# One tile shape for the attention sum's last four matmuls, and a new search in the planner that orders an attention and two-layer MLP kernel

## The chip, the cores and the metric

One NeuronCore of a Trainium2 chip runs the whole program. The metric is the device time of one execution in microseconds (us). The profiled execution is another one, with its own time, and its trace gives start and length of every instruction.

## The reference

Thresholded attention over 4 batches x 8 heads, 576 queries and keys, head size 64, then two MLPs over 2304 tokens (512 wide, 2048 hidden). All in float32.

```python
scores = q @ k.T / 8
scores = where(scores >= max(scores) - tau, scores, -1e9)
x = softmax(scores) @ v                      # 2304 x 512
h = x @ w_in;  x = (max(h, 0) + log1p(exp(-abs(h)))) @ w_out    # first MLP
h = x @ w2_in; out = max(h, 0)**2 @ w2_out                      # second MLP
```

## The kernel before

**Tiles.** The attention is cut into 32 units. A unit is two heads of one half of a batch's queries (288 queries); four units make one token group of 288 tokens, and there are eight groups. The first MLP works on a group at a time in eight steps of 256 hidden columns (`m1_up`, `m1_split`, `m1_down`), 12 slots behind the attention (LAG). The second MLP follows in blocks of 512 tokens.

**Numbers in two parts.** A product in the MLPs is made of three matmuls of type float32r: high part by high part, low by high, high by low (L463 to L465 up, L494 to L496 down, L603 to L605 in the second MLP). The parts are split by ScalarE (a copy to float32r) and by DVE or GpSimd (the difference: L324 for weights, L344 and L345 for q and k, L482 for the hidden activations). The attention's products of weights and values stay float32; each of those matmuls shows up in the trace as two passes.

**A unit on TensorE.** `a_scores` makes the scores (L364 with 64 rows, two heads side by side; L369 with all rows). After the threshold and exp (`a_max`, `a_soft`, on DVE and ScalarE) `a_out` sums: L420 multiplies by v into `X`, 64 columns a head; L427 multiplies by ones (`one_t`, 32 columns) into `D`, which gives the denominators. Both run over 512 keys. The last 64 keys of the two heads share one 128-row slot of the tile, so the last piece of `a_out` has four matmuls of 64 rows each, in the order L432, L433, L432, L433:

```python
for o, h in enumerate(half):      # half: rows 0-63, rows 64-127
    PE.matmul(X[h], vt[h, 512:], e[h, 4], start=False, stop=True)
    PE.matmul(D[64 - 64 * o:96 - 64 * o], one_t[h], e[h, 4], start=False, stop=True)
```

L432 has 64 rows by 64 columns, L433 64 rows by 32 columns. `X` and `D` are two PSUM banks. Rows 0-63 write partitions 0-63 of `X` and 64-95 of `D`; rows 64-127 write partitions 64-127 of `X` and 0-31 of `D`. In this text these four are the slot.

**The planner.** Nothing is issued when it is written. `P.add` records an operation with its engine, an assumed duration in ns, what it reads and writes, and a key. `emit` turns the records into one order per engine: `forward` lists them by key as they come free, `backward` lists them from the end and gives new keys, and the two take turns 24 times; the shortest plan is issued. Each engine then takes its instructions strictly in that order. A flag `lock` says that GpSimd's work and some DVE work exclude each other in the plan. `emit` is called twice: once for attention with the first MLP's first 57 up steps, once for the rest. The assumed time of the slot is 590 ns, that of L420 and L427 is 490 ns a piece, with 100 more for a first piece.

Of the kernel before, what the change touches and what calls it, by code (L numbers as in the profile page):

```python
# [2 lines left out]

# [6 lines left out]
F32 = mybir.dt.float32  # L10
# [3 lines left out]
ALU = mybir.AluOpType  # L14
AX = mybir.AxisListType

B, H, S, D = 4, 8, 576, 64
# [9 lines left out]
LAG = 12  # L27
# [5 lines left out]
GPOOL = range(8, 56)  # L33
# [4 lines left out]
def f32(ap):  # L38
    return ap.bitcast(F32)


class Plan:
# [24 lines left out]
        deps.discard(i)  # L67
        self.ops.append((eng, ns, fn, deps, key, nbytes, lock or eng == "POOL"))

    def emit(self, rounds=24):  # L70

        first, n = len(self.done), len(self.ops)
        state = self.free, self.bus, self.lock
        self.done += [None] * (n - first)
        users = [[] for _ in range(n - first)]
        for i in range(first, n):  # L80
            for d in self.ops[i][3]:
                if d >= first:
                    users[d - first].append(i)
        keys = [op[4] for op in self.ops[first:]]
        best = None
        for r in range(rounds):
            self.free, self.bus, self.lock = dict(state[0]), *state[1:]
            order = self.forward(first, users, keys)
            length = max(self.free.values())
            if best is None or length < best[0]:  # L90
                best = length, order, self.done[first:], (self.free, self.bus, self.lock)
            keys = self.backward(first, users, order)
        _, order, self.done[first:], (self.free, self.bus, self.lock) = best
        for _, _, i in order:
            self.ops[i][2]()
# [122 lines left out]
def kernel(ctx: ExitStack, tc: tile.TileContext, qT, kT, vp, tau, w1i, w1o, w2i, w2o, out):  # L218
    nc = tc.nc
    w1i, w1o, w2i, w2o = (w.bitcast(U32) for w in (w1i, w1o, w2i, w2o))  # L220
    PE, ACT, DVE, POOL, SP = nc.tensor, nc.scalar, nc.vector, nc.gpsimd, nc.sync
# [35 lines left out]
    P = Plan()  # L257
    att = ExitStack()
    ap = att.enter_context(tc.tile_pool(name="att", bufs=1))
# [6 lines left out]
    k_h, k_l = (ap.tile([128, KW], F32R, name=f"k_{n}") for n in "hl")  # L266
# [7 lines left out]
    NX = 5  # L274
    xf_t = many(NX, [128, HALF], "xf")
    w_t = ap.tile([128, 18], F32, name="w_t")
    one_t = ap.tile([128, 32], F32, name="one_t")
    POOL.memset(one_t, 1.0)
    m_d = [dram.tile([18, 32], F32, name=f"m_d{i}") for i in range(4)]


# [4 lines left out]
    class Weights:  # L286
# [7 lines left out]
        def load(self, src, f, outw, key=None, pe=False):  # L294
            s = self.i % self.n
            self.i += 1
            raw, t = self.raw[s], self.t[s]
            R, T = ("wraw", id(self), s), ("wt", id(self), s)
            p, j = divmod(f, 2)
            hi, lo = (woh, wol) if outw else (wih, wil)  # L300
            W = ("wo" if outw else "wi", p, j)
            if outw:
                P.add("SP", 600, lambda: SP.dma_start(raw.rearrange("p e w -> p (e w)"), src[f * 128:(f + 1) * 128, :]), [], [R], key, 1 << 19)
                hf, lf, t2 = hi[p][:, j], lo[p][:, j], t
            else:
                P.add("SP", 600, lambda: SP.dma_start(raw.rearrange("p e w -> p (e w)"), src[f]), [], [R], key, 1 << 19)
                hf, lf = (x[p][:, :, 128 * j:128 * j + 128] for x in (hi, lo))
                t2 = t.rearrange("p (k f) -> p k f", k=4)
            low, high = raw[:, :, 0], raw[:, :, 1]
            P.add("ACT", 560, lambda: ACT.activation(f32(t), f32(high), AF.Prelu, scale=2.0 ** -112, alpha=-2.0 ** 32), [R], [T], key)  # L310
            P.add("DVE", 340, lambda: DVE.tensor_scalar(low, low, 29, None, op0=ALU.logical_shift_right), [], [R], key, lock=True)
            P.add("DVE", 610, lambda: DVE.scalar_tensor_tensor(out=t, in0=t, scalar=3, in1=low, op0=ALU.logical_shift_left, op1=ALU.bitwise_or), [R], [T], key, lock=True)
            P.add("ACT", 510, lambda: ACT.copy(hf, f32(t2)), [T], [W], key)
            if pe:
                bank, BK = h_ps[self.i // 2 % 2], ("h", self.i // 2 % 2)

                def mms():
                    PE.matmul(bank, ident, f32(t), start=True, stop=False)
                    PE.matmul(bank, negid, hf, start=False, stop=True)
                P.add("PE", 1300, mms, [T, W], [BK], key)  # L320
                b2 = bank if outw else bank.rearrange("p (k f) -> p k f", k=4)
                P.add("ACT", 530, lambda: ACT.copy(lf, b2), [BK], [W], key)
                return
            P.add("POOL", 1240, lambda: POOL.tensor_tensor(lf, f32(t2), f32(hf), op=ALU.subtract), [T], [W], key)  # L324


    def a_load(u, key):
# [10 lines left out]
    def a_prep(u, key):  # L338
        if u < RAW:
            return  # L340
        k_r, q_r, KR, QR = k_rt[u % 2], q_rt[u % 2], ("k_r", u % 2), ("q_r", u % 2)
        P.add("ACT", 330, lambda: ACT.copy(q_h, q_r), [QR], ["q_h"], key)
        P.add("ACT", 630, lambda: ACT.copy(k_h, k_r), [KR], ["k_h"], key)
        P.add("POOL", 750, lambda: POOL.tensor_tensor(q_l, q_r, f32(q_h), op=ALU.subtract), [QR, "q_h"], ["q_l"], key)  # L344
        P.add("POOL", 1520, lambda: POOL.tensor_tensor(k_l, k_r, f32(k_h), op=ALU.subtract), [KR, "k_h"], ["k_l"], key)  # L345

    def a_scores(u, key):

# [59 lines left out]
    def a_out(u, key):  # L408
        cold = COLD if u < NCOLD else 1
        e, E = st_t[u % 3], [("st", u % 3, o) for o in range(2)]  # L410
        vt, V = v_t[u % 2], ("v", u % 2)
        xf, XF = xf_t[u % NX], ("xf", u % NX)
        rb, RB = rb_t[0], "rb"
        half = [slice(0, 64), slice(64, 128)]
        X, D = a_ps[0][:, :HALF], a_ps[1][:, :HALF]
        AX0, AD = ("a", 0), ("a", 1)
        for c in range(4):
            def mms(c=c):
                for o in range(2):
                    PE.matmul(X[64 * o:64 * o + 64], vt[:, 256 * o + 64 * c:256 * o + 64 * c + 64], e[:, 5 * o + c], start=(c == 0), stop=False)  # L420
            P.add("PE", (490 + 100 * (c == 0)) * cold, mms, E + [V], [AX0], key)
        for c in range(0, 4, 2):
            def mms(c=c):
                for o in range(2):
                    for i in range(2):
                        a = 64 - 64 * o + 32 * i
                        PE.matmul(D[a:a + 32], one_t, e[:, 5 * o + c + i], start=(c == 0), stop=(c == 2 and i == 1))  # L427
            P.add("PE", (490 + 100 * (c == 0)) * cold, mms, E, [AD], key)

        def mms():  # L430
            for o, h in enumerate(half):
                PE.matmul(X[h], vt[h, 512:], e[h, 4], start=False, stop=True)  # L432
                PE.matmul(D[64 - 64 * o:96 - 64 * o], one_t[h], e[h, 4], start=False, stop=True)  # L433
        P.add("PE", 590 * cold, mms, [E[0], V], [AX0, AD], key)
        P.add("ACT", 310, lambda: ACT.copy(xf, X), [AX0], [XF], key - 0.5)
        for o in range(2):
            P.add("ACT", 310, lambda o=o: ACT.copy(rb[half[o]], D[half[1 - o]]), [AD], [RB], key - 0.5)

        d, DN = d_t[u % 2], ("d", u % 2)
        P.add("DVE", 380, lambda: DVE.tensor_reduce(d[:, 0], rb.rearrange("p (b i) -> p b i", i=32), axis=AX.X, op=ALU.max, apply_transpose=True), [RB], [DN], key + 1)  # L440
        for a in range(4):
            b = a ^ 1
            P.add("ACT", 220, lambda a=a, b=b: ACT.copy(d[32 * a:32 * a + 32, 1], d[32 * b:32 * b + 32, 0]), [DN], [("d2", u % 2)], key + 0.5)
        P.add("DVE", 140, lambda: DVE.scalar_tensor_tensor(out=d[:, 0], in0=d[:, 0], scalar=1e-9, in1=d[:, 1], op0=ALU.add, op1=ALU.add), [("d2", u % 2)], [DN], key + 1)
        P.add("DVE", 140, lambda: DVE.reciprocal(d[:, 0], d[:, 0]), [], [DN], key + 1)
        P.add("DVE", 380, lambda: DVE.transpose(rb, d[:, 0].unsqueeze(2).to_broadcast([128, 9, 32])), [DN], [RB], key + 1)
        P.add("DVE", 375, lambda: DVE.tensor_tensor(xf, xf, rb, op=ALU.mult), [RB], [XF], key + 1, lock=True)
# [28 lines left out]
            P.add("DVE", 370, lambda j=j, h=h, a=a: DVE.scalar_tensor_tensor(out=gt_t[j], in0=h, scalar=0.0, in1=a, op0=ALU.max, op1=ALU.add), [("h", j), A], [("gt", j)], key - 0.2)  # L476

    def m1_split(key):
        eng, e, ns = ("POOL", POOL, 750) if key - LAG in GPOOL else ("DVE", DVE, 375)
        for j in range(2):  # L480
            P.add("ACT", 330, lambda j=j: ACT.copy(g_hl[0][j], gt_t[j]), [("gt", j)], [("g_h", j)], key - 0.2)  # L481
            P.add(eng, ns, lambda j=j: e.tensor_tensor(g_hl[1][j], gt_t[j], f32(g_hl[0][j]), op=ALU.subtract), [("gt", j), ("g_h", j)], [("g_l", j)], key - 0.2, lock=True)  # L482
# [211 lines left out]
```

## Time and profile before

| | |
|---|---|
| median of 3 runs | 1174.6 us (1174.29 to 1176.4) |
| the profiled execution's own time | 1177.02 us |
| its span, first to last instruction | 1175.2 us |
| TensorE (PE) busy | 1145.8 us, 98% |
| DVE busy | 698.6 us, 59% |
| ScalarE (ACT) busy | 690.8 us, 59% |
| GpSimd (POOL) busy | 245.6 us, 21% |
| granted TensorE clock, mean | 0.988 |

The profiled execution lies 2.4 us over the median. A busy share is a mean over the span; the attention ends at about 706 us, and DVE, ScalarE and GpSimd do most of their work before that. A matmul is listed with its whole length, and the next begins before it ends, so what a matmul costs TensorE is read as the time from its start to the next one's start.

### The profile page before, as it was taken

Reading aid. Unit: us, or ns where it says so; the run is one execution under the profiler, and the core shown is the slowest. Engines: PE = TensorE matmul, PEld = TensorE weight load, DVE = VectorE, ACT = ScalarE, POOL = GpSimd, SP = SyncE. Lnnn points to the kernel's source line nnn. Section 1 sums busy time; section 2 is a strip of 40 time slices with the busy share of each in tenths; the row PEclk is TensorE's granted clock in tenths of the full one; section 3 lists DMA queues with packets and bytes.
Section 4 is the critical chain, followed back from the end, with each engine's and each line's share of the span. In section 5 each row is a group of like instructions: output and inputs, shape, how many; then the busy total and the mean of one; then the engine's idle time right before and its main releaser. Section 6 shows DMA issues by size and latency. Waiting matters only on the chain.

```text
span 1175.2 us, 18185 instructions
## 1 busy us (share of the span) xinstructions
PE 1145.8 (98%) x6992; PEld 887.8 (76%) x6992; DVE 698.6 (59%) x992; ACT 690.8 (59%) x1640; POOL 245.6 (21%) x209
## 2 busy tenths in 40 slices
PE   7779999999999999999999999999999999999998
PEld 3335777877877877877777879988888888888887
DVE  5999986766776666657656745889322322222232
ACT  6787887777777776777677657865322222222222
POOL 1024223332332232333223211444000000000000
PEclk9888999999999999999999999999999999999999
DMA  5365422112112112112111004765010010000010
GB/s 190 109 200 181 140 89 84 46 44 81 46 39 83 41 45 83 39 48 74 47 48 42 31 11 146 212 205 159 7 66 1 1 54 1 1 37 1 1 37 19
DMA packets 39291, 81.85 MB, mean 70 GB/s; under 512 B 6180, under 2 KB 14884, under 8 KB 39204
## 3 DMA queue, kind: packets, MB, share of 16 engines
q1 hardware_dynamic: 39204, 80.69, 21.6%
q8 instruction: 55, 0.90, 0.3%
q14 instruction: 32, 0.26, 0.1%
HBM read 71.17 MB, written 9.50 MB: 69 GB/s over the span
## 4 chain that ended last, share of the span: by engine, by line
PE 90%; DVE 4%; ACT 3%; DMA 1%; issue 0%; SPq 0%; ACTq 0%; DVEq 0%
PE h_ps L463 12%; PE h_ps L464 11%; PE h_ps L465 11%; PE y_ps L494 6%; PE y_ps L604 6%; PE y_ps L603 6%; PE y_ps L605 6%; PE y_ps L496 5%; PE y_ps L495 5%; PE a_ps L364 5%; PE a_ps L420 5%; PE a_ps L432 3%; PE a_ps L433 3%; PE a_ps L427 3%; DVE st L402 1%; PE a_ps L369 1%
## 5 line engine op out<-in xcount | busy, mean ns | idle before, releaser
L482 POOL TENSOR_TENSOR g_l<-gt,g_h 128x288 fp32r<-128x288 f32 x96 | 102.8, 1074 | 316.4 <-ACT g_h L481 278.8
L463 PE MATMUL h_ps<-x_h,wih 128*128 128x288 f32 x512 | 160.1, 313 | 0.7 <-DVE gt L476 0.7
L494 PE MATMUL y_ps<-g_h,woh 128*128 128x288 f32 x512 | 158.2, 309 | 0.0
L464 PE MATMUL h_ps<-x_l,wih 128*128 128x288 f32 x512 | 150.5, 294 | 1.2 <-DVE x_l L454 1.2
L465 PE MATMUL h_ps<-x_h,wil 128*128 128x288 f32 x512 | 151.6, 296 | 0.0
L496 PE MATMUL y_ps<-g_l,woh 128*128 128x288 f32 x512 | 151.1, 295 | 0.0
L495 PE MATMUL y_ps<-g_h,wol 128*128 128x288 f32 x512 | 150.9, 295 | 0.0
L402 DVE TENSOR_TENSOR st<-st,mb 64x288 f32<-64x288 f32 (+1 forms) x128 | 129.0, 1022 | 3.3 <-DMA mb<-m_d 2.2
L583 ACT ACTIVATE r<-h_ps 128x512 f32<-128x512 f32 (+1 forms) x80 | 44.5, 556 | 146.2 <-PE h_ps L465 145.8
L584 DVE SCALAR_TENSOR_TENSOR r<-h_ps,r 128x512 f32<-128x512 f32 (+1 forms) x80 | 51.0, 638 | 131.8 <-ACT r L583 131.6
L464 PE MATMUL h_ps<-y_l,wih 128*128 128x512 f32 (+1 forms) x320 | 120.1, 375 | 0.1
L590 ACT CAST g_h<-r 128x512 fp32r<-128x512 f32 (+1 forms) x80 | 46.2, 578 | 125.4 <-PE y_ps L604 125.4
L463 PE MATMUL h_ps<-y_h,wih 128*128 128x512 f32 (+1 forms) x320 | 119.2, 372 | 0.0
L465 PE MATMUL h_ps<-y_h,wil 128*128 128x512 f32 (+1 forms) x320 | 118.7, 371 | 0.0
L591 DVE TENSOR_TENSOR g_l<-r,g_h 128x512 fp32r<-128x512 f32 (+1 forms) x80 | 51.7, 646 | 110.9 <-ACT g_h L590 110.8
L604 PE MATMUL y_ps<-wol,g_h 128*128 128x512 f32 x288 | 114.1, 396 | 0.0
L603 PE MATMUL y_ps<-woh,g_h 128*128 128x512 f32 x288 | 114.1, 396 | 0.0
L605 PE MATMUL y_ps<-woh,g_l 128*128 128x512 f32 x288 | 114.0, 396 | 0.0
L463 PEld LDWEIGHTS h_ps<-x_h,wih 128*128 128x128 f32 x512 | 96.4, 188 | 21.9 <-issue 18.7
L494 PEld LDWEIGHTS y_ps<-g_h,woh 128*128 128x128 f32 x512 | 96.4, 188 | 16.4 <-issue 15.3
L405 DVE SCALAR_TENSOR_TENSOR st<-st,thr 128x1152 f32<-128x1152 f32 (+1 forms) x64 | 104.1, 1628 | 0.1
L476 DVE SCALAR_TENSOR_TENSOR gt<-h_ps,a_t 128x288 f32<-128x288 f32 x128 | 57.4, 450 | 77.3 <-ACT a_t L475 73.9
(102 smaller groups left out, 2410.5 us busy)
## 6 DMA issues: line engine op xcount, KB each, us to landing
k_r<-in_kT SPq DMA_DIRECT2D x32, 320.0 KB
v_t<-in_vp SPq DMA_DIRECT2D x32, 288.0 KB
wraw<-in_w1i SPq DMA_DIRECT2D x16, 512.0 KB
wraw<-in_w1o SPq DMA_DIRECT2D x16, 512.0 KB
wraw<-in_w2i SPq DMA_DIRECT2D x16, 512.0 KB
wraw<-in_w2o SPq DMA_DIRECT2D x16, 512.0 KB
mb<-m_d SPq DMA_DIRECT2D x28, 288.0 KB
q_r<-in_qT SPq DMA_DIRECT2D x32, 144.0 KB
```

Source lines behind the costliest of these rows:

```text
L402: DVE.tensor_tensor(st[p0:p1, a:a + n], st[p0:p1, a:a + n], mb[p0:p1, o:o + 1].to_broadcast([p1 - p0, n, HALF]), op=ALU.subtract),
L405: P.add("DVE", 315 * (s1 - s0), lambda x=x: DVE.scalar_tensor_tensor(out=x, in0=x, scalar=thr, in1=x, op0=ALU.is_lt, op1=ALU.subtract), [] ...
L463: PE.matmul(bank, wih[p][:, c, f], xh[c], start=(c == 0), stop=False)
L464: PE.matmul(bank, wih[p][:, c, f], xl[c], start=False, stop=False)
L465: PE.matmul(bank, wil[p][:, c, f], xh[c], start=False, stop=(c == 3))
L482: P.add(eng, ns, lambda j=j: e.tensor_tensor(g_hl[1][j], gt_t[j], f32(g_hl[0][j]), op=ALU.subtract), [("gt", j), ("g_h", j)], [("g_l", j)] ...
L494: PE.matmul(o, woh[p][:, j, es], g_h[j], start=first, stop=False)
L495: PE.matmul(o, wol[p][:, j, es], g_h[j], start=False, stop=False)
L496: PE.matmul(o, woh[p][:, j, es], g_l[j], start=False, stop=last)
L603: PE.matmul(o, g_h[j][:, ts], woh[p][:, j], start=first, stop=False)
L604: PE.matmul(o, g_h[j][:, ts], wol[p][:, j], start=False, stop=False)
L605: PE.matmul(o, g_l[j][:, ts], woh[p][:, j], start=False, stop=last)
```

## The change

Three edits. The ones tile has 64 columns, the second 32 of them zero. L427 takes the first 32 columns. In the slot the sum for `D` takes all 64, so all four matmuls are 64 rows by 64 columns, and 64 partitions of `D` are written where 32 were. The planner's assumed times for GpSimd go up, and that of L420 is divided a little differently. The planner takes 150 rounds; at every eighth it goes back to the best order so far and adds random numbers with a spread of 1500 ns to the keys.

```diff
-    def emit(self, rounds=24):
+    def emit(self, rounds=150):
...
-        best = None
+        best, rnd = None, random.Random(1)
...
-            keys = self.backward(first, users, order)
+            keys = self.backward(first, users, order if r % 8 else best[1])
+            if r % 8 == 0 and r:
+                keys = [k + rnd.gauss(0, 1500) for k in keys]
...
-    one_t = ap.tile([128, 32], F32, name="one_t")
-    POOL.memset(one_t, 1.0)
+    one_t = ap.tile([128, 64], F32, name="one_t")
+    POOL.memset(one_t, 0.0)
+    POOL.memset(one_t[:, :32], 1.0)
...
-            P.add("POOL", 1240, lambda: POOL.tensor_tensor(lf, f32(t2), f32(hf), op=ALU.subtract), [T], [W], key)
+            P.add("POOL", 1500, lambda: POOL.tensor_tensor(lf, f32(t2), f32(hf), op=ALU.subtract), [T], [W], key)
...
-        P.add("POOL", 750, lambda: POOL.tensor_tensor(q_l, q_r, f32(q_h), op=ALU.subtract), [QR, "q_h"], ["q_l"], key)
-        P.add("POOL", 1520, lambda: POOL.tensor_tensor(k_l, k_r, f32(k_h), op=ALU.subtract), [KR, "k_h"], ["k_l"], key)
+        P.add("POOL", 1000, lambda: POOL.tensor_tensor(q_l, q_r, f32(q_h), op=ALU.subtract), [QR, "q_h"], ["q_l"], key)
+        P.add("POOL", 1630, lambda: POOL.tensor_tensor(k_l, k_r, f32(k_h), op=ALU.subtract), [KR, "k_h"], ["k_l"], key)
...
-            P.add("PE", (490 + 100 * (c == 0)) * cold, mms, E + [V], [AX0], key)
+            P.add("PE", (484 + 105 * (c == 0)) * cold, mms, E + [V], [AX0], key)
...
-                        PE.matmul(D[a:a + 32], one_t, e[:, 5 * o + c + i], start=(c == 0), stop=(c == 2 and i == 1))
+                        PE.matmul(D[a:a + 32], one_t[:, :32], e[:, 5 * o + c + i], start=(c == 0), stop=False)
...
-                PE.matmul(D[64 - 64 * o:96 - 64 * o], one_t[h], e[h, 4], start=False, stop=True)
+                PE.matmul(D[64 - 64 * o:128 - 64 * o], one_t[h], e[h, 4], start=False, stop=True)
...
-        eng, e, ns = ("POOL", POOL, 750) if key - LAG in GPOOL else ("DVE", DVE, 375)
+        eng, e, ns = ("POOL", POOL, 1000) if key - LAG in GPOOL else ("DVE", DVE, 375)
```

In the changed kernel the lines from L283 on have numbers higher by 4 (L436 and L437 are the slot's L432 and L433). The search gives another order on every engine, in both parts. Two places show what moves.

The first place is TensorE's order around the 15th unit's `a_out`. Before, its 16 matmuls over the 512 keys stand in two blocks ahead of the slot (`a_ps_146<-..one_t` is `D`, `a_ps_145<-..v_t` is `X`):

```order
L369 MATMUL a_ps_145<-q_h,k_h 128x288
L369 MATMUL a_ps_145<-q_h,k_l 128x288
L369 MATMUL a_ps_145<-q_l,k_h 128x288
L427 MATMUL a_ps_146<-st_159,one_t 32x288 x8
L420 MATMUL a_ps_145<-st_159,v_t_147 64x288 x8
L432 MATMUL a_ps_145<-st_159,v_t_147 64x288
L433 MATMUL a_ps_146<-st_159,one_t 32x288
L432 MATMUL a_ps_145<-st_159,v_t_147 64x288
L433 MATMUL a_ps_146<-st_159,one_t 32x288
L463 MATMUL h_ps_68<-x_h_126,wih_74 128x288
```

In the changed kernel:

```order
L424 MATMUL a_ps_145<-st_159,v_t_147 64x288 x4
L498 MATMUL y_ps_66<-g_h_131,woh_89 128x288
L499 MATMUL y_ps_66<-g_h_131,wol_97 128x288
L500 MATMUL y_ps_66<-g_l_133,woh_89 128x288
L498 MATMUL y_ps_66<-g_h_132,woh_89 128x288
L499 MATMUL y_ps_66<-g_h_132,wol_97 128x288
L500 MATMUL y_ps_66<-g_l_134,woh_89 128x288
L424 MATMUL a_ps_145<-st_159,v_t_147 64x288 x2
L436 MATMUL a_ps_145<-st_159,v_t_147 64x288
L437 MATMUL a_ps_146<-st_159,one_t 64x288
L436 MATMUL a_ps_145<-st_159,v_t_147 64x288
L437 MATMUL a_ps_146<-st_159,one_t 64x288
```

The pieces of this unit's `a_out` have full-size matmuls of the first MLP between them; in some other units, the 16th and the 20th among them, they still stand in one block. The slot's four stand together in every unit, in the same order as before.

The second place is DVE's order ahead of the last of the four differences `x_l` that open the second token group (L454, `x_l_130`), before:

```order
L402 TENSOR_TENSOR st_159<-st_159,mb_164 128x1152
L444 SCALAR_TENSOR_TENSOR d_168<-d_168 128x9
L482 TENSOR_TENSOR g_l_133<-gt_137,g_h_131 128x288
L445 RECIPROCAL d_168<-d_168 128x9
L402 TENSOR_TENSOR st_159<-st_159,mb_164 64x288
L446 STREAM_TRANSPOSE rb_166<-d_168 128x288
L402 TENSOR_TENSOR st_159<-st_159,mb_164 64x288
L447 TENSOR_TENSOR xf_173<-xf_173,rb_166 128x288
L405 SCALAR_TENSOR_TENSOR st_159<-st_159,thr 128x1440
L454 TENSOR_TENSOR x_l_130<-xf_173,x_h_126 128x288
```

In the changed kernel (L458 is L454):

```order
L458 TENSOR_TENSOR x_l_127<-xf_175,x_h_123 128x288
L450 STREAM_TRANSPOSE rb_166<-d_168 128x288
L409 SCALAR_TENSOR_TENSOR st_159<-st_159,thr 128x1440
L451 TENSOR_TENSOR xf_173<-xf_173,rb_166 128x288
L480 SCALAR_TENSOR_TENSOR gt_138<-h_ps_68,a_t_136 128x288
L458 TENSOR_TENSOR x_l_128<-xf_171,x_h_124 128x288
L458 TENSOR_TENSOR x_l_129<-xf_172,x_h_125 128x288
L315 TENSOR_SCALAR wraw_186<-wraw_186 128x512
L315 TENSOR_SCALAR wraw_187<-wraw_187 128x512
L316 SCALAR_TENSOR_TENSOR wt_188<-wt_188,wraw_186 128x512
L458 TENSOR_TENSOR x_l_130<-xf_173,x_h_126 128x288
```

The instruction stands almost as deep in DVE's queue as before: counted over the whole queue ahead of it, one wide L402 and one wide L405 more, one L312 and one L482 fewer.

## Rows read from the trace of the kernel before

**Rows 1.** Busy time by stretch: engine busy us (count), granted clock, DMA share, GB/s.
```profile
30.00:60.00 30.00, 24.03 (x139) 9.49 (x139) 29.62 (x40) 23.20 (x56) 2.55 (x2) 0.90 0.36 117
60.00:90.00 30.00, 23.78 (x99) 10.87 (x96) 29.05 (x44) 26.80 (x69) 5.97 (x4) 0.83 0.64 207
120.00:150.00 30.00, 30.00 (x214) 23.16 (x213) 27.56 (x48) 26.37 (x64) 7.14 (x5) 1.00 0.50 147
150.00:200.00 50.00, 49.26 (x367) 36.74 (x366) 40.69 (x59) 39.83 (x102) 16.13 (x13) 1.00 0.22 74
400.00:500.00 100.00, 100.00 (x725) 76.01 (x723) 64.56 (x90) 71.16 (x187) 32.55 (x28) 1.00 0.19 58
900.00:1000.00 100.00, 100.00 (x429) 80.43 (x428) 27.83 (x39) 24.92 (x39) 0.00 (x0) 1.00 0.05 16
```

**Rows 2.** Chain that ended last, last unit's sum: start us, length us, what.
```profile
700.26 2.09 PE a_ps L420 x16
702.36 1.11 PE a_ps L427 x16
703.46 0.63 PE a_ps L432 x2
704.09 0.60 PE a_ps L433 x2
704.69 0.63 PE a_ps L432 x2
705.32 0.60 PE a_ps L433 x2
705.91 0.33 PE h_ps L463
```

**Rows 3.** Groups of instructions by line and shape, the slot's two lines.
```profile
L432 PE MATMUL a_ps<-st,v_t 64*64 64x288 f32 x128 | 44.5, 428 | 0.0
L433 PE MATMUL a_ps<-st,one_t 64*32 64x288 f32 x128 | 42.8, 415 | 0.0
```

**Rows 4.** Timeline of PE around a scores piece: start us, length us, what.
```profile
408.88 0.29 PE L464 MATMUL h_ps<-x_l,wih 128*128 128x288 f32 x1
409.01 0.29 PE L465 MATMUL h_ps<-x_h,wil 128*128 128x288 f32 x1
409.23 0.40 PE L364 MATMUL a_ps<-q_h,k_h 64*128 64x288 f32 x2
409.47 0.29 PE L364 MATMUL a_ps<-q_h,k_l 64*128 64x288 f32 x2
409.60 0.29 PE L364 MATMUL a_ps<-q_l,k_h 64*128 64x288 f32 x2
409.82 0.40 PE L463 MATMUL h_ps<-x_h,wih 128*128 128x288 f32 x1
```

**Rows 5.** Timelines of DVE, then of PE, where the second group begins.
```profile
189.85 0.45 DVE L454 TENSOR_TENSOR x_l<-xf,x_h 128x288 fp32r<-128x288 f32 x1
...
191.80 0.29 PE L464 MATMUL h_ps<-x_l,wih 128*128 128x288 f32 x1
```

**Rows 6.** Groups of instructions by line and shape, DVE and POOL.
```profile
L402 DVE TENSOR_TENSOR st<-st,mb 128x1152 f32<-128x1152 f32 x64 | 90.9, 1439 | 2.3 <-DMA mb<-m_d 2.2
L405 DVE SCALAR_TENSOR_TENSOR st<-st,thr 128x1152 f32<-128x1152 f32 x32 | 47.5, 1484 | 0.1
L312 DVE SCALAR_TENSOR_TENSOR wt<-wt,wraw 128x512 uint32<-128x512 uint32 x64 | 66.3, 1037 | 2.2 <-ACT wt L310 1.5
L482 DVE TENSOR_TENSOR g_l<-gt,g_h 128x288 fp32r<-128x288 f32 x32 | 20.1, 634 | 4.9 <-ACT g_h L481 4.8
L482 POOL TENSOR_TENSOR g_l<-gt,g_h 128x288 fp32r<-128x288 f32 x96 | 102.8, 1074 | 316.4 <-ACT g_h L481 278.8 <-PE y_ps L496 16.6 <-DVE d L440 7.9
```

**Rows 7.** DVE's waits from 110 to 191 us: total us, times, longest.
```profile
DVE mr L384 <- ACT r L383: 3.1, 2, 2.2
DVE d L444 <- ACT d L443: 3.0, 2, 2.4
DVE d L440 <- ACT rb L437: 2.1, 2, 1.4
DVE g_l L482 <- ACT g_h L481: 1.3, 2, 1.2
```

**Rows 8.** Chain that ended last, where the second MLP begins.
```profile
718.41 2.07 DMA y_d<-wraw
...
733.80 2.29 DVE y_l L573
736.13 0.50 PE h_ps L464
```

More of the change, by code (lines that the diff above doesn't have):

```diff
@@ L1 @@
 import heapq
+import random
 from contextlib import ExitStack
```

## Prediction

> **What bounds the kernel now.** I read the busy times by stretch first. From 120 us on TensorE is busy without a gap, 100.00 of 100.00 us between 400 and 500 us, while ScalarE stands at 71 and DVE at 65 [rows 1]. So from there the end is TensorE's own work: whatever it no longer has to do moves the end, until something else is late. The start is different. From 30 to 90 us DVE is busy 29.62 and 29.05 of 30 us, TensorE only about 24, at a granted clock of 0.90 and 0.83. DVE still has 27.56 of 30 in the stretch from 120 us and 40.69 of 50 in the one from 150 us. DVE's queue sets the pace at the start and is close behind until about 190 us.
>
> Next, what TensorE's work consists of. In the chain through the last unit's sum, the 16 passes of L420 take 2.09 us, the 16 of L427 1.11, and the slot 705.91 - 703.46 = 2.45 us for eight passes [rows 2]. The reader should see that the slot, with a quarter of the two blocks' passes, takes three quarters of their time. The two blocks give the price of a pass. L420 has two column halves side by side, so eight passes one behind the other and the cost s of coming into another tile shape; L427 has four column quarters, so four passes and s. From 8p + s = 2.09 and 4p + s = 1.11 follow p = 0.245 and s = 0.13 us. The slot's lines then read as 2p + s = 0.62 each, four times over: shown are 0.63, 0.60, 0.63, 0.60. So nothing runs together in the slot now, and each of its four matmuls pays for a change of shape, since 64 by 64 and 64 by 32 alternate.
>
> **The change, part by part.**
>
> *The slot.* All four matmuls get one shape, and their row and column halves are four different quarters of the array. If all run together, the slot is 2p + s = 0.62 us, 1.83 less. There are 128 passes on each of L432 and L433 [rows 3], so 64 matmuls on each line and 32 slots: 32 x 1.83 = 58.6 us of TensorE work. The trace has no four quarters at work together. The bounds: the slot stays at 2.45 (every quarter waits for the one before), or it falls to 0.62. I take 0.62, since it is nearest to what the rows show: column parts run together in L420 and L427 although both write one bank, and row halves do in the scores: L364's pairs, each two heads, follow each other at 0.13 us, the step of one single full-size matmul, L464 to L465 [rows 2, 4].
>
> The row halves of L364 write two different banks. In the slot each bank gets output from both row halves, on different partitions. The Trainium skill (TensorEngine Tiling (Array Packing), Restrictions and Gotchas) says that different row tiles can't access the same PSUM bank at once. No row here shows that case. By that rule the slot would go in two turns; that is rival 2.
>
> *The ones' wider tile and the memsets.* 64 columns of `D` instead of 32 add zeros to partitions that are never late: the same passes, the same length. One memset more on GpSimd at the start, far ahead of its first use: nothing. Were it not covered, it would be some 0.1 us, about what a small instruction takes.
>
> *The order on TensorE.* I counted changes of tile shape along TensorE's order: 463 before, of which 96 lie inside the slots and are paid for in the 2.45; 367 remain. Now there are 427, none inside a slot, because pieces of `a_out` are spread among the MLP's matmuls, as at the 15th unit. Of the 60 more, 41 lead into float32 pieces, at 0.13 each. The other 19 lead into float32r work; there L465 to L364 takes 0.22 instead of 0.13, and the first pair 0.24 instead of 0.13, so 0.19 with rounding [rows 4]. Together 41 x 0.13 + 19 x 0.19 = 8.9 us more work. TensorE's sum is 58.6 - 8.9 = 49.7 us smaller.
>
> *What of that lands.* In the start DVE sets the pace, and there TensorE only waits longer. The place to look at is the last `x_l` that opens the second token group. DVE ends it at 190.3 us, and TensorE first reads it at 191.80: hardly late now [rows 5]. After the change TensorE would be there some 11 us sooner (8 slots less, 16 more changes of shape). DVE wouldn't: ahead of this instruction in its queue stand one L402 and one L405 more, one L312 and one L482 fewer, 1.44 + 1.48 - 1.04 - 0.63 = 1.2 us more [rows 6], so it comes at 191.5. Some of DVE's idle time before it will go, since part of it goes back to TensorE through ScalarE: from 110 to 191 us it is 3.1 + 3.0 + 2.1 + 1.3 = 9.5 us [rows 7]. I take 3 of these 9.5; the bounds are none and all. So TensorE goes on at 188.5 instead of 191.8, 3.3 sooner. Behind this place lie 24 slots in both orders, 24 x 1.83 = 43.9 us less, and 44 more changes of shape (25 and 19), 25 x 0.13 + 19 x 0.19 = 6.9 more. That makes 3.3 + 43.9 - 6.9 = 40.3 us sooner.
>
> *What is late next.* Two small things against it. Where the second MLP begins, a chain of the last store (718.41), the weights' load and DVE's `y_l` ends at 736.1, and TensorE's wait there is already open by about half a us, the L464 of 0.50 instead of 0.23 [rows 8]. Between that store's group and the first matmul of the second MLP TensorE now has 0.8 us less to do (six 128-row matmuls fewer at 0.13): I count 1 us. And between 200 and 700 us a unit takes about 8% less on TensorE, so ScalarE goes from 71% to about 77% busy [rows 1], in an order that allows for nothing late: I count 2 us of new waits, with none and 12 as bounds (half a us for each of some 23 units).
>
> *GpSimd's assumed times.* They change no duration. L482 takes 1.07 us on GpSimd [rows 6], and the planner had 0.75, now 1.00. Its orders should come true more often; that is worth nothing that I can count, and it is why I leave the new waits at 2.
>
> **The sum.** 40.3 - 1 - 2 = 37.3 us. The profiled execution took 1177.0 us, so 1139.7 for one like it; it lies 2.4 over the median of 1174.6. Against the median: 1137.3, and I give 1138.
>
> **The rivals.**
>
> 1. *All of it lands.* DVE gives back all its idle time or finds a better packing, and TensorE is early from the first units on. For it: 150 rounds instead of 24. Against it: DVE has under 1 us in 30 free from 30 to 90 us, and its work is the same. 1174.6 - 49.7 = 1125. Chance 0.10.
>
> 2. *The slot goes in two turns.* Where two row halves write one bank, the second pair waits: 4p + s = 1.11 us, as L427's four passes. The slot then saves 1.34 and not 1.83, which behind the place is 24 x 0.49 = 11.8 us less gain: 1149. For it: no row shows two row halves in one bank. Against it: the two halves never write the same partitions. Chance 0.15.
>
> 3. *ScalarE's queue becomes the bound between 200 and 700 us.* A late copy or exponential makes TensorE wait in each unit; at half a us a unit 12 instead of 2 us, with the slot at 0.62: 1148. For it: the old order had 1.83 us a unit of hidden slack, since the slot took 2.45 where the plan had 0.59, and that slack goes. Against it: 23% of ScalarE remains free. Chance 0.10.
>
> 4. *Slower: the slot stays at 2.45 and the new order only adds changes of shape.* This is the case if going to another quarter drains the array as a change of shape does. TensorE then stays the bound at the place, and 6.9 to 8.9 us of added changes land: 1182. It decides from the slot's second matmul on: if its start lies 0.6 us behind the first's, this is it. For it: the four stand one by one today. Against it: column halves and row halves each run together. Chance 0.05.
>
> 5. *The slot goes one by one, but without changes of shape*, 8p + s = 2.09 us. 24 x 0.36 = 8.6 us less against 6.9 more: no change that shows, about 1174. The change would then not do what it says. Chance 0.04.
>
> **How the numbers follow.** The forecast has 0.56. Its own range is 1128 to 1146: DVE's idle time between all and none is 6.5 us sooner or 3 us later, the new waits run up to 6. To hold 8 in 10 the range reaches down to rival 1 and up past rivals 2 and 3, 1124 to 1158. Outside lie rivals 4 and 5 (0.09), and some tenth for rivals 2 and 3 together. A difference of 0.2%, 2.3 us, is about what a measurement of this kernel can tell from none. Faster by more than that: the forecast, rivals 1 to 3 and a little of rival 5, 0.92. Slower: rival 4, 0.05. The rest, 0.03, is no change.
>
> **What would show it.** Right: the slot's eight passes from first start to the next instruction's at about 0.6 us, all four matmuls starting within some ten ns; the attention's end about 35 us sooner; TensorE with some 10 us more idle time before 190 us than now, and next to none from 200 to 700 us. Two groups of starts half a us apart would be rival 2, gaps ahead of TensorE with ScalarE as the releaser after 200 us rival 3. The forecast is wrong as a whole if the slot isn't below 1.2 us, or if the second group's last `x_l` ends later than 195 us.

## The result, and the profile after

| | before | after |
|---|---|---|
| median of the runs, us | 1175.5 (4 runs, 1174.29 to 1177.79) | 1136.4 (4 runs, 1135.64 to 1138.96) |
| the profiled execution, us | 1177.02 | 1135.64 |
| span, us | 1175.2 | 1133.7 |
| TensorE busy, us | 1145.8 | 1096.8 |
| span less TensorE busy, us | 29.4 | 36.9 |

The ratio is 0.967, with an interval from 0.965 to 0.969: 39 us, 3.3% faster. 1138 was forecast, with 1124 to 1158 around it.

The changed kernel's page, busy time by engine:

```profile
PE 1096.8 (97%) x6992; PEld 870.0 (77%) x6992; DVE 687.7 (61%) x992; ACT 684.7 (60%) x1640; POOL 249.9 (22%) x210
```

TensorE is busy 49.0 us less, where its work was to shrink by 49.7. It is idle 7.5 us more. The stretches say where; these answer to [rows 1]:

```profile
30.00:60.00 30.00, 22.64 (x125) 8.19 (x125) 29.18 (x39) 24.56 (x61) 5.07 (x2) 0.84 0.41 127
60.00:90.00 30.00, 22.22 (x114) 9.34 (x110) 28.43 (x43) 24.31 (x61) 5.64 (x4) 0.78 0.57 180
150.00:200.00 50.00, 50.00 (x398) 39.89 (x395) 39.07 (x67) 42.11 (x114) 13.95 (x13) 1.00 0.32 92
400.00:500.00 100.00, 100.00 (x789) 79.02 (x785) 74.79 (x103) 76.34 (x201) 37.02 (x30) 1.00 0.20 61
650.00:700.00 50.00, 47.88 (x349) 42.83 (x349) 24.65 (x48) 33.73 (x81) 9.62 (x10) 0.97 0.35 113
```

From 30 to 90 us TensorE is busy 44.9 us where it was 47.8, behind a DVE that is nearly as full as before (57.6 of 60 us, 58.7 before). Between 400 and 500 us it stays without a gap, at 789 matmuls where there were 725, and ScalarE stands at 76. One new hole lies between 650 and 700 us; before, this stretch had none:

```profile
650.00:700.00 50.00, 50.00 (x370) 41.14 (x368) 33.30 (x47) 33.15 (x80) 11.03 (x12) 1.00 0.06 19
```

The slot, on TensorE's timeline of the changed kernel, where [rows 2] had 2.45 us:

```profile
464.62 0.41 PE L424 MATMUL a_ps<-st,v_t 128*64 128x288 f32 x2
464.96 0.45 PE L436 MATMUL a_ps<-st,v_t 64*64 64x288 f32 x1
464.97 0.45 PE L437 MATMUL a_ps<-st,one_t 64*64 64x288 f32 x1
464.97 0.45 PE L436 MATMUL a_ps<-st,v_t 64*64 64x288 f32 x1
464.98 0.45 PE L437 MATMUL a_ps<-st,one_t 64*64 64x288 f32 x1
465.25 0.40 PE L436 MATMUL a_ps<-st,v_t 64*64 64x288 f32 x1
...
465.61 0.40 PE L498 MATMUL y_ps<-g_h,woh 128*128 128x288 f32 x1
```

Four matmuls start within 20 ns, four more (their second passes) 0.29 us later, and the next instruction follows 0.65 us after the first: all four quarters run at once.

### The profile page after: what moved, and what is told of

Same layout as the page of the kernel before. It is cut to its first block, busy times and chain, and to the rows that moved or that the text cites. A ratio compares the mean times of both kernels' runs of the same rounds, so it can differ in the third digit from the quotient of the medians.

```text
span 1133.7 us, 18190 instructions
## 1 busy us (share of the span) xinstructions
PE 1096.8 (97%) x6992; PEld 870.0 (77%) x6992; DVE 687.7 (61%) x992; ACT 684.7 (60%) x1640; POOL 249.9 (22%) x210
## 4 chain that ended last, share of the span: by engine, by line
PE 90%; ACT 5%; DVE 2%; DMA 1%; issue 1%; POOL 0%; SPq 0%; ACTq 0%; DVEq 0%
PE h_ps L467 13%; PE h_ps L469 12%; PE h_ps L468 12%; PE y_ps L498 7%; PE y_ps L607 6%; PE y_ps L608 6%; PE y_ps L609 6%; PE y_ps L500 6%; PE y_ps L499 6%; PE a_ps L368 6%; PE a_ps L424 6%; PE a_ps L431 3%; PE a_ps L436 1%; ACT st L376 1%; ACT st L410 1%; PE a_ps L373 1%
## 5 line engine op out<-in xcount | busy, mean ns | idle before, releaser
L486 POOL TENSOR_TENSOR g_l<-gt,g_h 128x288 fp32r<-128x288 f32 x96 | 100.1, 1045 | 284.8 <-ACT g_h L485 225.1
L498 PE MATMUL y_ps<-g_h,woh 128*128 128x288 f32 x512 | 160.5, 313 | 0.0
L406 DVE TENSOR_TENSOR st<-st,mb 64x288 f32<-64x288 f32 (+1 forms) x128 | 126.2, 1000 | 3.1 <-DMA mb<-m_d 2.1
```

What stands on the lines that cost most here:

```text
L406: DVE.tensor_tensor(st[p0:p1, a:a + n], st[p0:p1, a:a + n], mb[p0:p1, o:o + 1].to_broadcast([p1 - p0, n, HALF]), op=ALU.subtract),
L498: PE.matmul(o, woh[p][:, j, es], g_h[j], start=first, stop=False)
```

## The experiments

All were timed beside the kernel before, which had medians of 1174.8 to 1176.7 us in those series. Changes of shape are counted along TensorE's order; those inside the slots are left out.

| kernel | changes of shape | median us | ratio, interval | PE busy | span less PE busy |
|---|---|---|---|---|---|
| the change | 427 | 1136.4 | 0.967 (0.965 to 0.969) | 1096.8 | 36.9 |
| 1 shape alone | 367 | 1126.1 | 0.958 (0.956 to 0.960) | 1088.7 | 36.0 |
| 2 order alone | 427 | 1184.1 | 1.007 (1.004 to 1.009) | 1153.6 | 30.2 |
| 3 slot in pairs | 367 | 1143.4 | 0.972 (0.971 to 0.974) | 1109.9 | 31.8 |
| 4 24 rounds | 382 | 1132.9 | 0.964 (0.962 to 0.966) | 1093.8 | 37.6 |
| 5 GpSimd's old times | 445 | 1137.6 | 0.967 (0.966 to 0.969) | 1102.5 | 34.4 |
| 6 another seed | 419 | 1136.0 | 0.966 (0.965 to 0.968) | 1097.2 | 36.3 |
| 7 shape priced, 24 rounds | 365 | 1131.4 | 0.962 (0.961 to 0.964) | 1090.5 | 38.8 |
| 8 shape priced, 150 rounds | 360 | 1129.3 | 0.961 (0.959 to 0.963) | 1088.9 | 38.3 |
| 9 noise by unit | 383 | 1128.3 | 0.959 (0.957 to 0.961) | 1091.6 | 35.7 |
| 10 late store | 427 | 1137.2 | 0.967 (0.965 to 0.968) | 1098.5 | 37.8 |
| 11 sums whole | 359 | 1128.8 | 0.960 (0.958 to 0.962) | 1088.1 | 39.2 |
| 12 8 and 9 together | 357 | 1127.5 | 0.959 (0.957 to 0.961) | 1086.7 | 38.9 |

**1. The shape alone.** The kernel before with these lines; its planner is as it was, and so is its order.

```diff
-    one_t = ap.tile([128, 32], F32, name="one_t")
-    POOL.memset(one_t, 1.0)
+    one_t = ap.tile([128, 64], F32, name="one_t")
+    POOL.memset(one_t, 0.0)
+    POOL.memset(one_t[:, :32], 1.0)
...
-                PE.matmul(D[64 - 64 * o:96 - 64 * o], one_t[h], e[h, 4], start=False, stop=True)
+                PE.matmul(D[64 - 64 * o:128 - 64 * o], one_t[h], e[h, 4], start=False, stop=True)
```

> The kernel before with the one tile shape alone; its order and the planner's times and rounds stay. Theory (the slot's shape is the gain, and the new order costs TensorE some 9 us of added changes of shape): the slot takes 0.62 to 0.65 us, there are 367 changes of shape, and the time is 1128 to 1138 us, no slower than the change as a whole. Rival (the new GpSimd times and the search are needed to make use of the shorter slot, since the old order was never in time with GpSimd): new waits on TensorE after 200 us, 1145 us or more.

1126.1 us, 2 us under the range that I gave: the whole gain is in the shape, and this version beats both kernels. Its slot takes the same 0.65 us (461.01 to 461.66). TensorE's busy time falls by 57.1 us, of the 58.6 worked out for 32 slots, and 6.6 us go into more idle time. The rest of the change takes 10 us away again.

**2. The order alone.** The changed kernel with `one_t` of 32 columns and the slot's old lines.

```diff
-                PE.matmul(D[64 - 64 * o:128 - 64 * o], one_t[h], e[h, 4], start=False, stop=True)
+                PE.matmul(D[64 - 64 * o:96 - 64 * o], one_t[h], e[h, 4], start=False, stop=True)
```

> The changed kernel with the slot's old shapes (64 by 64 and 64 by 32 in turn) in its new order. Theory: the slot stays at 2.45 us and the 60 more changes of shape cost what was worked out, so 1180 to 1185 us, some 0.6% slower than before. Rival (the new order is worth something by itself, in the start): 1175 us or less.

1184.1 us, slower than before by 0.7% and clear of the noise. The slot reads as it did, in the chain that ended last:

```profile
445.93 0.63 PE a_ps L435 x2
446.55 0.60 PE a_ps L436 x2
447.15 0.63 PE a_ps L435 x2
447.78 0.60 PE a_ps L436 x2
```

TensorE is busy 7.8 us more than before. The 60 added changes of shape were worked out as 8.9. With experiment 1 this is the difference from both sides: the new order costs 8.1 us of TensorE's busy time with the new slot (1096.8 less 1088.7), and 7.8 with the old. Not all of it is changes of shape: this order also has a hole with a slow stretch behind it, here at 727 us (experiment 10 has it for the changed kernel).

**3. The slot in pairs.** The kernel before with the two L432 first and the two L433 behind them, shapes as they were.

```diff
             for o, h in enumerate(half):
                 PE.matmul(X[h], vt[h, 512:], e[h, 4], start=False, stop=True)
+            for o, h in enumerate(half):
                 PE.matmul(D[64 - 64 * o:96 - 64 * o], one_t[h], e[h, 4], start=False, stop=True)
```

> The kernel before with the slot's four matmuls put as L432, L432, L433, L433: the two row halves of one bank stand together, in one shape. Theory (row halves run together even in one bank, so long as their partitions differ and the shape is one): each pair takes about 0.62 us, the slot 1.25, the time is some 30 to 39 us under before, 1137 to 1147. Rival (two row halves of one bank take turns): each pair takes about 1.1 us, the slot 2.2, the time is 1165 to 1170.

1143.4 us. TensorE's timeline:

```profile
446.57 0.66 PE L420 MATMUL a_ps<-st,v_t 128*64 128x288 f32 x4
447.16 0.70 PE L432 MATMUL a_ps<-st,v_t 64*64 64x288 f32 x4
447.79 0.68 PE L434 MATMUL a_ps<-st,one_t 64*32 64x288 f32 x4
448.40 0.40 PE L464 MATMUL h_ps<-x_h,wih 128*128 128x288 f32 x1
```

Each pair, four passes, takes 0.63 and 0.61 us, as long as one matmul alone did. Both matmuls of a pair write one bank, from different row halves and on different partitions, and run together. So the slot's trouble before was the alternation of shapes, and the rule of the Trainium skill (TensorEngine Tiling (Array Packing), Restrictions and Gotchas), that different row tiles can't access one PSUM bank at once, doesn't hold here where the partitions differ. A reordering of two lines without any wider tile gives some 32 of the 49 us.

**4 to 6. Which part of the planner.** Experiment 4 is the changed kernel with `rounds=24` and without the restarts. Experiment 5 keeps the search and takes back GpSimd's four assumed times. Experiment 6 is `random.Random(2)`.

> The changed kernel with 24 rounds and no restarts; the shape and GpSimd's new times stay. Its order has 382 changes of shape in place of 427. Theory (TensorE's work after the start decides, and the long search buys nothing that the chip sees): about 7 us less work on TensorE, 1127 to 1135 us. Rival (the search shortens the start or takes out waits): 1140 us or more.

> The changed kernel with GpSimd's old assumed times (750, 750, 1520, 1240 ns); the one shape and the 150 rounds with restarts stay. Its order has 445 changes of shape, 18 more than the changed kernel, 78 more than the kernel with the shape alone. Theory (an order with restarts costs by its changes of shape, and GpSimd's assumed times matter little): 3 us over the changed kernel, 1137 to 1143 us. Rival (the right GpSimd times are what a good order hangs on): 1150 us or more.

> The changed kernel with another seed for the restarts. Its order has 419 changes of shape, 8 fewer. Theory (random keys pull pieces of one tile shape apart whatever the seed): 1133 to 1139 us, and in any case over the shape alone with its old order by 5 us or more. Rival (the changed kernel's order was a bad draw): 1129 us or less.

All three times lie in the first theory's ranges, 1132.9, 1137.6 and 1136.0 us. The work behind them fits less well: experiment 4 has 45 changes of shape fewer and 3.0 us less busy time where about 7 were expected, and 5 has 18 more and 5.7 us more. Listed busy time differs between orders by more than the changes of shape, and what else goes into it was not taken apart. GpSimd's assumed times move the result by about 1 us, which the intervals can't tell from nothing. With a spread of 0 in place of 1500 the planner's 150 rounds end at the very order of experiment 4 (an order worked out, not timed): more rounds alone find nothing, and what the restarts change is random.

**9. Random numbers by unit.** The changed kernel with

```diff
-                keys = [k + rnd.gauss(0, 1500) for k in keys]
+                by = {}
+                keys = [k + by.setdefault((op[4], op[0]), rnd.gauss(0, 1500)) for k, op in zip(keys, self.ops[first:])]
```

> The changed kernel with the restarts' random numbers drawn once for all operations of one engine that were recorded with the same key, and not for each operation. Pieces of one unit's sum then move together; the order has 383 changes of shape in place of 427. Theory (it is the random number for each piece that pulls pieces of one shape apart): 44 fewer changes, 6 to 7 us less, 1127 to 1133 us. Rival (the search is slower for another reason): 1136 us or more.

1128.3 us, 8.1 under the change, with 44 changes of shape fewer and 5.2 us less TensorE busy time. So it is the random number for each single piece that scatters a unit's sum.

**7, 8 and 12. A planner that knows the price.** In 7 (on the kernel of experiment 1) and 8 (on the changed kernel), each TensorE piece is recorded without a change of shape, and both directions of the planner add it; 8 also prefers a ready piece of the shape at hand. 12 is 8 with 9.

```diff
+            if eng == "PE":
+                if self.shapes[i] != self.last:
+                    ns += 190 if self.shapes[i] < 3 else 135
+                self.last = self.shapes[i]
```

> The kernel before with the one shape, 24 rounds, GpSimd's old assumed times, and a planner that knows the change of shape: every TensorE piece is recorded without it, and 190 ns (into float32r) or 135 ns (into float32) are added where the piece before has another shape. Its order has 365 changes of shape (367 with the shape alone). Theory (what TensorE has to do is what counts after the start): the same work, so within 4 us of the shape alone, 1122 to 1130 us. Rival (a plan with truer TensorE times also shortens the start): 1120 us or less.

> The changed kernel (150 rounds, restarts, GpSimd's new assumed times) with the planner that knows the change of shape, and that takes a ready piece of the shape at hand where its key is no more than 3000 ns later. Its order has 360 changes of shape in place of 427. Theory (the search lost its gain to changes of shape alone): 67 fewer are 10 to 11 us, so 1122 to 1128 us. Rival (the search's orders are slower for another reason, such as a longer start): 1131 us or more.

> The changed kernel with both remedies: random numbers once for all operations of one engine recorded with the same key, and the planner that knows the change of shape and prefers the shape at hand within 3000 ns. Its order has 357 changes of shape, 10 fewer than the kernel before with the shape alone. Theory (TensorE's work decides, and the long search is no worse in the start): 1120 to 1128 us, at or under the shape alone with 1126. Rival (the start of each order differs by several us whatever its changes of shape, and the shape alone had a good one): 1129 to 1134 us.

1131.4, 1129.3 and 1127.5 us. 7 and 8 lie 1 us over the theory's range; 12 lies inside it, but not at or under the shape alone, as that theory had it. 8 is 7.1 us under the change, with 7.9 us less busy time. Against experiment 1, busy time is 1090.5, 1088.9 and 1086.7 us where that has 1088.7, and the idle time is 2 to 3 us longer. None of them beats the shape alone: 7 is slower than it, and 8 and 12 can't be told from it.

**11. Sums in whole blocks.** Experiment 1 with the four pieces of L420 recorded as one operation, and the two of L427 as one.

```diff
-            P.add("PE", (490 + 100 * (c == 0)) * cold, mms, E + [V], [AX0], key)
+        P.add("PE", 2060 * cold, mms, E + [V], [AX0], key)
```

> The kernel before with the one shape, and with the four pieces of L420 recorded as one operation and the two of L427 as one, so that nothing comes between them; 24 rounds, GpSimd's old assumed times. Its order has 359 changes of shape (367 with the shape alone). Theory (fewer changes of shape are less work): 1 us less than the shape alone, 1121 to 1127 us. Rival (a sum in whole blocks can't fill TensorE's small gaps and frees its banks later, so that the start or the steady stage gets longer): 1129 us or more.

1128.8 us: a miss of the theory, 2 us over its range and just under the rival's. Busy time fell by 0.6 us, where 1 was expected, and idle time grew by 3.2.

**10. The hole at 675 us.** The changed kernel's timelines of TensorE and its windows show the hole, and what followed it:

```profile
677.03 0.56 PE L467 MATMUL h_ps<-x_h,wih 128*128 128x288 f32 x1 [2.12 <-DVE gt L480]
```

```profile
673.00:677.00 4.00, 1.92 (x15) 1.68 (x13) 1.30 (x4) 2.94 (x8) 0.00 (x0) 1.00 0.41 152
677.00:681.00 4.00, 3.97 (x18) 3.97 (x19) 1.17 (x3) 0.88 (x3) 0.00 (x0) 0.57 0.62 188
681.00:685.00 4.00, 4.00 (x32) 4.00 (x31) 1.79 (x4) 2.34 (x6) 0.00 (x0) 1.00 0.90 349
```

After 2.1 us of waiting the granted clock is 0.57 in the next 4 us, between the two levels, 1.2 and 2.4 GHz, and 18 matmuls start where 32 do a little later. My theory was ScalarE's order: two copies of the first MLP's store stood ahead of the activation functions. The edit puts them behind, in the finished order (`hold` has the two copies, `at` their places, `end` the place of the sixth ScalarE operation behind them):

```diff
+            deps = set(self.hold)
+            moved, kept = [], []
+            for j in range(min(at), end + 1):
+                i = seq[j]
+                if i in self.hold or self.ops[i][3] & deps:
+                    deps.add(i)
+                    moved.append(i)
+                else:
+                    kept.append(i)
...
+            seq[min(at):end + 1] = kept + moved
```

> The changed kernel with two instructions moved in the finished order: ScalarE's two copies that store half of token group 7's sums (L507) stand behind the next step's six activation functions, and not ahead of them; the store's DMA follows them. Theory (these copies wait in ScalarE's queue for TensorE's last sum, and the activation functions that TensorE needs wait behind them): TensorE's gap of 2.1 us at 675 us shrinks below 0.8, the granted clock does not fall behind it, and the time falls by 2 to 4 us, 1132 to 1135. Rival (the gap has another cause, such as the DMA or DVE): the gap and the time stay.

The time stayed, 1137.2 us, and so did the hole. TensorE's and ScalarE's timelines of this kernel:

```profile
679.45 0.41 PE L487 MATMUL h_ps<-x_h,wih 128*128 128x288 f32 x1 [2.12 <-DVE gt L500]
```

```profile
674.26 0.43 ACT L477 CAST x_h<-xf 128x288 fp32r<-128x288 f32 x1 [1.23 <-DVE xf L471]
676.97 0.87 ACT L497 ACTIVATE a_t<-h_ps 128x288 f32<-128x288 f32 x2 [2.27 <-PE h_ps L489]
677.74 0.77 ACT L498 ACTIVATE a_t<-a_t 128x288 f32<-128x288 f32 x2
678.40 0.76 ACT L499 ACTIVATE a_t<-a_t 128x288 f32<-128x288 f32 x2
```

With the copies out of the way, the activation functions wait for TensorE's last up matmul instead. My theory fell. What the rows show is a chain: TensorE ends one step's up matmuls, then three activation functions and `gt` must pass, and TensorE's next instruction in order is the next step's first up matmul, which waits for that `gt`. No other matmul stands between them in this order. The order makes the hole, not the slot: experiment 2 has it too, and experiment 6 has none. TensorE's timeline of experiment 2:

```profile
727.06 0.40 PE L466 MATMUL h_ps<-x_h,wih 128*128 128x288 f32 x1 [2.11 <-DVE gt L479]
```

In experiment 6's order 15 down matmuls stand between the two steps' up matmuls (669.0 to 671.0 us), and TensorE does not stop:

```profile
650.00:700.00 50.00, 50.00 (x391) 47.08 (x384) 26.11 (x50) 36.83 (x88) 8.89 (x9) 1.00 0.30 100
```

This fits the reading; an order that differs in nothing else was not tried.

## Why the prediction was right, step by step

**The slot: right.** 0.62 us forecast, 0.65 measured; 57.1 us of busy time in experiment 1 for 58.6 worked out. Rivals 2, 4 and 5 fell with the first timeline, and experiment 3 shows why rival 2 had to.

**The changes of shape: right behind the place.** Counted out along TensorE's order, the matmul that first reads the last `x_l` starts at 183.7 us after the change and at 191.4 before (I had named the one at 191.80, a later reader; 0.4 us). In experiments 1 and 2 it starts at 183.8 and 190.9. From there to the end it is 983.8 us before, 940.9 in experiment 1, 992.9 in experiment 2 and 950.0 after the change: the new order costs 9.1 us with either slot. Of these 0.7 and 0.8 are idle time. Some 1.7 are the slow stretch behind the hole, an estimate from 4 us at a granted clock of 0.57 (0.59 in experiment 2). The rest, 6.6 to 6.7 us, stands for 44 added changes, worked out as 6.9. Up to the place, where TensorE often waits, the other 16 can't be read off.

**Behind the place: right.** The 950.0 us are 33.8 less than the 983.8. The forecast was 43.9 - 6.9 less 3 of new waits, 34.0. Of the waits, ScalarE cost nothing that shows between 400 and 500 us, so rival 3 fell, and none over 0.15 us shows where the second MLP begins; instead it is the hole at 675 us and the low clock after it, a chain that I had not named. That these came to about the 3 us that I had set aside for others is luck.

**Up to the place: the term that was mis-sized.** I let TensorE go on 3.3 us sooner: DVE's queue 1.2 us longer, 3 of 9.5 us of idle time gone. DVE's timeline after the change:

```profile
182.25 0.46 DVE L458 TENSOR_TENSOR x_l<-xf,x_h 128x288 fp32r<-128x288 f32 x1 [0.50 <-ACT x_h L457]
```

It ends at 182.7, not 188.5, and TensorE was there 7.7 us sooner. Which part of the change did it is read from the four kernels that pair the old and the new slot with the old and the new order. Up to the end of this instruction, for the kernel before, experiment 1, experiment 2 and the change (TensorE's busy time comes first, DVE's third):

```profile
0.00:190.31 190.31, 165.88 (x952) 102.27 (x953) 165.97 (x235) 151.68 (x375) 46.00 (x39) 0.93 0.46 145
0.00:182.70 182.70, 152.04 (x952) 97.73 (x953) 165.81 (x235) 151.34 (x375) 45.34 (x40) 0.91 0.49 151
0.00:189.87 189.87, 165.45 (x947) 98.41 (x947) 159.45 (x235) 151.93 (x374) 47.36 (x37) 0.94 0.47 145
0.00:182.70 182.70, 151.81 (x947) 94.80 (x947) 158.98 (x235) 151.88 (x374) 46.66 (x38) 0.91 0.48 151
```

The same from 110 us on:

```profile
110.00:190.31 80.31, 79.83 (x570) 60.95 (x570) 70.65 (x109) 66.44 (x166) 26.11 (x18) 1.00 0.37 113
110.00:182.70 72.70, 71.74 (x550) 57.21 (x547) 69.47 (x108) 64.44 (x161) 23.40 (x17) 1.00 0.41 121
110.00:189.87 79.87, 79.87 (x565) 61.72 (x563) 67.89 (x109) 67.20 (x167) 25.21 (x16) 0.98 0.38 114
110.00:182.70 72.70, 72.61 (x562) 58.98 (x558) 65.67 (x106) 65.75 (x162) 23.62 (x15) 1.00 0.41 121
```

| | last `x_l` ends | DVE busy to there | DVE idle to there | of that, idle from 110 us on |
|---|---|---|---|---|
| before | 190.3 | 166.0 | 24.3 | 9.7 |
| 1 shape alone | 182.7 | 165.8 | 16.9 | 3.2 |
| 2 order alone | 189.9 | 159.5 | 30.4 | 12.0 |
| the change | 182.7 | 159.0 | 23.7 | 7.0 |

The new slot brings the place 7 to 8 us forward in either order, and does it through DVE's idle time alone: 7.4 us of it go in the old order, 6.7 in the new one, and DVE's work stays as it is. So the term that I set at 3 was about 7; of the 9.5 us that I had counted from 110 us on, 6.4 went with the old order. TensorE's rows say why. From 110 us on it is idle for 0.5 us before and for 0.1 us after the change, so its own work was the bound there already; the three slots in this stretch are worth 3 x 1.83 = 5.5 us, and the rest was not traced further. The prediction had the row (30.00 of 30.00 us from 120 us on) and let DVE's queue set the pace until 190 us all the same: that step was wrong.

The new order moved the place by 0.4 us with the old slot and not at all with the new one, where I had counted 1.2 us later. It shortens DVE's work by 6.5 to 6.8 us and lengthens DVE's idle time by about as much. The same instructions are shorter. Two groups of DVE's, up to 191 us before, and up to 183.5 us after the change and in experiment 1:

```profile
L482 DVE TENSOR_TENSOR g_l<-gt,g_h 128x288 fp32r<-128x288 f32 x15 | 10.0, 678 | 1.3 <-ACT g_h L481 1.3
L447 DVE TENSOR_TENSOR xf<-xf,rb 128x288 f32<-128x288 f32 x8 | 6.7, 838 | 0.1
```

```profile
L486 DVE TENSOR_TENSOR g_l<-gt,g_h 128x288 fp32r<-128x288 f32 x15 | 7.6, 506 | 4.8 <-ACT g_h L485 4.6
L451 DVE TENSOR_TENSOR xf<-xf,rb 128x288 f32<-128x288 f32 x8 | 3.6, 447 | 0.0
```

```profile
L483 DVE TENSOR_TENSOR g_l<-gt,g_h 128x288 fp32r<-128x288 f32 x15 | 10.0, 678 | 0.0
L448 DVE TENSOR_TENSOR xf<-xf,rb 128x288 f32<-128x288 f32 x8 | 6.7, 838 | 0.1
```

In experiment 1, with the old order, they are as long as before. In experiment 5 DVE's work up to its last `x_l` is short with GpSimd's old assumed times as well (158.5 us), while experiment 6, with another seed, has 164.4: the shorter work comes from the search's draw and not from the assumed times.

A side remark of mine was off by the prediction's own prices: 8 slots less and 16 changes more, all into float32 pieces, are 8 x 1.83 - 16 x 0.13 = 12.6 us, not some 11. Nothing in the sum hangs on it.

**The sum.** Like for like, by the profiled executions, the change took off 41.4 us where the sum had 37.3: 4.4 us more than forecast up to the place and 0.2 less behind it. In medians it is 39.1, since the execution profiled before lies 1.5 us over its median and the one after 0.8 under. So part of the nearness of 1136.4 to 1138 is luck. Of the signs I had named, the slot came true; TensorE had 6.5 us more idle time up to the place, not 10, and the attention ended 40 us sooner (665.9 us in place of 705.9), not 35; both fit a place that came sooner than forecast.

What stays open is the start. The orders of experiments 7, 8, 11 and 12 have no more TensorE work than experiment 1, within 2 us, and are idle 2 to 3 us longer, most of it before 200 us in 7, 11 and 12 and behind 200 us in 8. Which draw of DVE's and GpSimd's order has a short start was not settled.

## What to carry to other kernels

Small matmuls that are to run side by side need one tile shape, not only different places in the array: two instructions padded with zeros cost nothing here and took 49 us off the time, and putting equal shapes together took off two thirds of that. Where the order is searched with random keys, draw them for whole units, or price what the engine charges between neighbours: keys for single pieces pulled runs of one shape apart, the plan could not see it, and either remedy took 7 to 8 us off the change. No search here beat the old order with the new shape. Split a change that does two things before crediting either: here one part earned more than the whole. Where a wait seems to go to one engine, run the parts of the change one by one and look at the same place in each: DVE's work became shorter here, and that moved next to nothing.

## What the runs showed of the hardware

In these traces a DVE `TENSOR_TENSOR` that reads two tensors in SBUF and a GpSimd one that reads two do not run side by side; the one that comes second stands until the other is done, and the trace counts its standing as busy time. It does not hold for every DVE instruction with two sources: L476, which reads one of its two from PSUM, began 21 times while GpSimd was at work and never took over 0.46 us. DVE and GpSimd in the kernel before:

```profile
151.44 1.54 DVE L447 TENSOR_TENSOR xf<-xf,rb 128x288 f32<-128x288 f32 x1
```

```profile
151.06 1.61 POOL L324 TENSOR_TENSOR wol<-wt,woh 128x512 fp32r<-128x512 f32 x1 [9.12 <-ACT woh L313]
```

GpSimd ends at 152.67, and DVE's instruction, 0.45 us long elsewhere, ends 0.31 us after that. Of the 23 of L447 and L482 before 191 us, eight are longer than 0.9 us. Each of the eight began while GpSimd was at work, and each ends 0.31 us after GpSimd's end. It goes the other way too, where DVE has one such instruction after another:

```profile
129.11 1.89 POOL L324 TENSOR_TENSOR wol<-wt,woh 128x512 fp32r<-128x512 f32 x1 [5.28 <-ACT woh L313]
```

```profile
129.08 0.77 DVE L482 TENSOR_TENSOR g_l<-gt,g_h 128x288 fp32r<-128x288 f32 x2
```

GpSimd began just after DVE's first of two L482 and took 1.89 us, where its next L324 took 1.30, while both of DVE's kept their 0.40 and 0.44. In the changed kernel one of the 24 such DVE instructions before 191 us is longer than 0.9 us. DVE's group means thus hold waiting that no idle time shows, and a sum of them, as mine, carries one order's collisions over to another.
